# An If/Else on TensorE around the two matmul parts of each expert step: 192 or 128 token slots

## The chip, the cores and the metric

One core of one Trainium2 chip runs the kernel. The metric is the device time of one execution in microseconds; three timed runs of the kernel before are given, and one more execution was profiled. Engine names in the rows: PE is TensorE's matmuls, PEld its weight loads, DVE is VectorE, ACT ScalarE, POOL GpSimd, SP SyncE. A name with q (PEldq, ACTq) is what that engine's sequencer does by itself: waits, register loads, branches. L12 is line 12 of the kernel.

## What is computed

An attention stage (1152 rows of 512), a dense feed-forward layer, and then a mixture of eight experts, of which this change touches only the last:

```python
logits = x @ w_gate                          # 1152 tokens, 8 experts
expert_idx = np.argmax(logits, axis=1)
...                                          # disp[e, slot] = x[i]: the tokens of an expert in order
h = np.maximum(np.einsum('ecd,edf->ecf', disp, w1), 0.0)     # 512 -> 1024
y = np.einsum('ecf,efd->ecd', h, w2)                          # 1024 -> 512
out[i] = gate_w[i] * y[expert_idx[i], pos[i]]
```

An expert may hold up to 288 tokens. Working the reference's routing on its own inputs (seed 0) gives 138, 114, 113, 171, 190, 182, 128 and 116 tokens for experts 0 to 7.

## The kernel before, in words

All matrix products are in fp32 or in three products of split fp32 values (`mm3`: high by high, high by low, low by high). The experts run one after the other, each in eight steps; a step takes 128 of the 1024 hidden columns. Every expert is computed for 192 slots (`NW` = 128 + 64), whatever its number of tokens; slots above 192 have a block of their own at the end, under an If on all engines (L1132), which runs only if some expert has more than 192 tokens.

In a step TensorE does:

- `up(e, i)`: four fp32 matmuls of the step's slice of `w1b` with the gathered tokens `X`, 192 columns wide, into one of three PSUM banks `u`. In the trace each of them is two matmul records with two weight loads, so eight of each.
- `down(d, c)`, three steps behind (`LAG` = 3): the relu of an earlier step, `ht`, times the slice of the second weight. `mm3` into `y` for slots 0 to 127 is three matmuls of 512 columns; two more go into `z`, for the 64 slots above 127.
- at some steps `prep`: transposes of the next expert's gathered tokens (L930) that VectorE copies into `X`.

ScalarE and VectorE turn `u` into `ht` (`relu`, L1061 and L1063), split the second weights of the next expert into high and low parts (`split`, L235 and L236), and scale the finished `y` and `z` (`put_out`), which GpSimd scatters to the output. SyncE loads weights two to three experts ahead. The order on each engine is the order in which the main loop at the end of the kernel records the calls; `fills` is a table of extra calls after a step's matmuls. `r_final` (in expert 0) writes `flag_i`, and `get_flags` (expert 3) loads it into a register on every engine for the If at L1132.

The waits between engines are put in by the framework from the tiles that instructions read and write. An instruction with more than one wait gets wait instructions of its own ahead of it (EVENT_SEMAPHORE in the rows).

Of the kernel before, what the change touches and what calls it, by code (L numbers as in the profile page):

```python
# [1 line left out]

# [7 lines left out]
F32 = mybir.dt.float32  # L10
F32R = mybir.dt.float32r
I32 = mybir.dt.int32  # L12
# [3 lines left out]
ALU = mybir.AluOpType  # L16
AX = mybir.AxisListType

P = 128
# [5 lines left out]
PW = 384  # L25
N1 = 64
NW = P + N1
# [12 lines left out]
LAG = 3  # L40
# [2 lines left out]
_C = {}  # L43
_off = 0
for _name, _w in (("ident", 128), ("ml", KW), ("ml0", KW), ("ms", 54), ("tri", 128),
                  ("rev", 8), ("tok", 18), ("iota", PW)):
    _C[_name] = (_off, _w)
    _off += _w
CW = _off
# [3 lines left out]
def constants():  # L53
    c = np.zeros((P, CW), np.float32)

    def put(name, a):
        o, w = _C[name]
        c[: a.shape[0], o:o + w] = a

    i = np.arange(P)  # L60
    put("ident", np.eye(P))
    q = (i % QB)[:, None]
    col = np.arange(KW)[None, :]
    ok = (col > q) & (col <= q + STRIDE)
    put("ml", np.where(ok, 0.0, -8e9))
    put("ml0", np.where(ok & (col >= STRIDE), 0.0, -8e9))
    c54 = np.arange(54)[None, :]
    ok = (q // 18 == c54 // 18) & (c54 % 18 <= q % 18)
    put("ms", np.where(ok, 0.0, -8e9))
    put("tri", (i[:, None] < i[None, :]) * 1.0)  # L70
    put("rev", np.broadcast_to(8.0 - np.arange(8), (P, 8)))
    tok = np.empty((P, 9, 2))
    tok[:, :, 0] = i[:, None]
    tok[:, :, 1] = P * np.arange(9)[None, :]
    put("tok", tok.reshape(P, 18))
    slot = np.full(PW, -1.0)
    slot[0:NW] = np.arange(NW)
    slot[2 * P:PW - 32] = NW + np.arange(P - 32)
    put("iota", np.broadcast_to(slot, (P, PW)))
    return c  # L80
# [3 lines left out]
def tile_kernel(ctx, tc, cap, q, k, v, w_in, w_out, w_gate, w1, w2, consts, out):  # L84
    nc = tc.nc
# [3 lines left out]
    E, _, F = w1.shape  # L89
# [8 lines left out]
    cst = ctx.enter_context(tc.tile_pool(name="cst", bufs=1))  # L98
    dram = ctx.enter_context(tc.tile_pool(name="dram", bufs=1, space=bass.MemoryType.DRAM))
    rp = ctx.enter_context(tc.tile_pool(name="rp", bufs=3))  # L100
# [11 lines left out]
    def C(name):  # L112
        o, w = _C[name]
        return cs[:, o:o + w]
# [7 lines left out]
    idx_g = cst.tile([P, 3, E], I32, name="idx_g")  # L122
    idx_o = cst.tile([P, 3, E], I32, name="idx_o")
    gate = cst.tile([P, 3, E], F32, name="gate")
    flag_i = cst.tile([1, 1], I32, name="flag_i")
    x2d = dram.tile([NT, DM], F32, name="x2d")

    pp = ctx.enter_context(tc.tile_pool(name="ps", bufs=1, space=bass.MemoryType.PSUM))
# [5 lines left out]
    def psum(tag):  # L134
        name = rings[tag].pop(0)
        rings[tag].append(name)
        return pp.tile([P, 512], F32, tag=name, name=tag, bufs=1)
# [108 lines left out]
    def l1_mm(g, tb, c, tag):  # L246
        s, o = 2 * (g % 2), P * c
        hp = psum(tag)
        for kk in range(KC):
            mm3(hp[:, 0:TB], whi[s][:, kk, o:o + P], wlo[s][:, kk, o:o + P],  # L250
                xhi[:, kk, tb * TB:(tb + 1) * TB], xlo[:, kk, tb * TB:(tb + 1) * TB], kk == 0, kk == KC - 1)
            if kk < KC - 1:
                yield
        yield hp[:, 0:TB]
# [35 lines left out]
    def first_up():  # L290
        for c in range(2):
            for hp in l1_mm(0, 0, c, "f"):
                if hp is not None:
                    copies.append((nc.vector.tensor_copy if c else nc.scalar.copy, hb[c], hp))
                yield


    with ExitStack() as actx:
# [212 lines left out]
        up = first_up()  # L511
# [21 lines left out]
        for i in range(NGR):  # L533
# [6 lines left out]
            n, part = groups[i][:2]  # L540
# [21 lines left out]
        z = NGR - VL  # L562
        up = l1_mm(0, 0, 2, "f")
# [15 lines left out]
        hp = next(up)  # L579
# [7 lines left out]
        up = l1_mm(0, 0, 3, "acc")  # L587
# [212 lines left out]
    def r_final():  # L800
        extra = ohs
        cp = psum("m")
        for j, o in enumerate([cum] + extra):
            nc.tensor.matmul(cp[:, 0:E], lhsT=ones, rhs=o, start=j == 0, stop=j == len(extra))
        f = rp.tile([1, E], F32, name="flag", bufs=1)
        nc.vector.tensor_scalar(f, cp[0:1, 0:E], float(NW), None, op0=ALU.is_gt)
        fs = rp.tile([1, 1], F32, name="flags", bufs=1)
        nc.vector.tensor_reduce(out=fs, in_=f, axis=AX.X, op=ALU.add)
        nc.vector.tensor_copy(flag_i, fs)
        r_slot_ids(idx_o, idx)  # L810
# [69 lines left out]
    for n in range(4, nseq - 4):  # L880
        g, tb, c = seq[n]
# [167 lines left out]
            out=out, out_offset=bass.IndirectOffsetOnAxis(ap=idx_o[:n, ch, e:e + 1], axis=0), in_=y[:n], in_offset=None,  # L1049
            bounds_check=NT - 1, oob_is_err=False)  # L1050

    def up(e, i, n=NW):
        hp = psum("u")
        for kk in range(KC):
            nc.tensor.matmul(hp[:, 0:n], lhsT=w1b[e % 3][:, kk, P * i:P * i + P], rhs=X[e % 2][:, kk, 0:n],  # L1055
                             start=kk == 0, stop=kk == KC - 1)
        return hp
# [6 lines left out]
                                           op0=ALU.max, op1=ALU.subtract)  # L1064
        return t

    def down(e, i, t, y0, y1):
        j, c = 2 * (e % 2) + i // 4, i % 4
        for y in ((y1, y0) if i == 7 else (y0, y1)):
            if y is y0:  # L1070
                mm3(y0, t[:, 0:P], t[:, 2 * P:3 * P], whi[j][:, c], wlo[j][:, c], i == 0, i == 7)
            else:
                if i < 7:
                    nc.tensor.matmul(y1, lhsT=t[:, P:2 * P], rhs=whi[j][:, c], start=i == 0, stop=False)
                nc.tensor.matmul(y1[:N1], lhsT=t[:, P:NW], rhs=wlo[j][:, c], start=False, stop=False)
                if i == 7:
                    nc.tensor.matmul(y1, lhsT=t[:, P:2 * P], rhs=whi[j][:, c], start=False, stop=True)
# [6 lines left out]
    flags = []  # L1084

    def get_flags():
        flags.append(nc.values_load(flag_i[0:1, 0:1], min_val=0, max_val=E))

    fills = {}

    def fill(e, i, *fs):
        fills.setdefault((e, i), []).extend(fs)

    fill(0, 0, (r_match, BB))
    fill(0, 1, (r_index, BA))
    fill(0, 2, (r_index, BB), (gather, 1, 0), (gather, 1, 1), (r_final,))
    fill(0, 3, (r_weigh, BA))
    fill(0, 4, (r_weigh, BB))
    for e in range(E):
        fill(e, 3 if e == 0 else 0, (gather, e + 2, 0))  # L1100
        fill(e, 4 if e == 0 else 1, (gather, e + 2, 1))
        for h in range(4):
            fill(e, SPLIT_AT[h], (split, e + 1, h))
        fill(e, 5, (prep, e + 1, 0))
        fill(e, 6, (prep, e + 1, 1))
        for j in range(2):
            fill(e, 3 + 4 * j, (w1load, e + 3, j))
    fill(3, 0, (get_flags,))

    r_match(BA)  # L1110
    PARTS = ((NW, P, N1), (NW + N1, 0, P))
    ht, ys = {}, {}
    for s in range(8 * E + LAG):
        e, i = divmod(s, 8)
        if s < 8 * E:
            hp = up(e, i)
        d, c = divmod(s - LAG, 8)
        if s >= LAG:
            if c == 0:
                ys[d] = psum("y"), psum("z")  # L1120
            down(d, c, ht.pop((d, c)), *ys[d])
        for f, *args in fills.pop((e, i), []):
            f(*args)
        if s < 8 * E:
            ht[e, i] = relu(hp, PARTS)
        if s >= LAG and c == 7:
            y0, y1 = ys.pop(d)
            put_out(d, 1, y1)
            put_out(d, 0, y0)
    assert not fills, fills  # L1130

    with tc.If(flags[0] > 0):  # L1132
        n = ROWS[2]
        for e in range(E):
# [11 lines left out]
            for i in range(8):  # L1146
                t = relu(up(e, i, n), ((n, 0, n),), n)
                j, c = 2 * (e % 2) + i // 4, i % 4
# [32 lines left out]
```

## Time and profile before

| | |
|---|---|
| timed runs | 485.38, 487.12, 490.08 us (median 487.12) |
| the profiled execution | 483.33 us, of which the profile's span is 481.5 us |
| TensorE busy | 95% of the span, 3053 matmuls |
| VectorE, ScalarE, GpSimd busy | 59%, 42%, 25% |
| mean granted TensorE clock | 0.974 of full speed |
| expert steps in the trace | from 303.5 us (first `up`) to 470.3 us (last `down`) |

The span is told in us from its first instruction. A matmul's record is longer than the time after which the next one starts, since matmuls overlap; how long one takes up the engine is read from start to start.

### The profile page before, as it was taken

Reading aid. Unit: us, or ns where it says so; the run is one execution under the profiler, and the core shown is the slowest. Engines: PE = TensorE matmul, PEld = TensorE weight load, DVE = VectorE, ACT = ScalarE, POOL = GpSimd, SP = SyncE. Lnnn points to the kernel's source line nnn. Section 1 sums busy time; section 2 is a strip of 40 time slices with the busy share of each in tenths; the row PEclk is TensorE's granted clock in tenths of the full one; section 3 lists DMA queues with packets and bytes.
Section 4 is the critical chain, followed back from the end, with each engine's and each line's share of the span. In section 5 each row is a group of like instructions: output and inputs, shape, how many; then the busy total and the mean of one; then the engine's idle time right before and its main releaser. Section 6 shows DMA issues by size and latency. Waiting matters only on the chain. (4 is left out here: it accounts for less than half of the span.)

```text
span 481.5 us, 8430 instructions
## 1 busy us (share of the span) xinstructions
PE 455.1 (95%) x3053; PEld 390.3 (81%) x3055; DVE 285.5 (59%) x785; ACT 203.8 (42%) x521; POOL 120.5 (25%) x152
## 2 busy tenths in 40 slices
PE   8989898999998989999999999999999999999990
PEld 4667677898887879887998888988888888888880
DVE  3676999357878855787325686654454454455210
ACT  4576787245463432534244143323343342423211
POOL 1323553012332320323054215420220303101001
PEclk9987999999999999999999999799999999999996
DMA  7989747014243650446034013998767677200000
GB/s 158 217 211 231 179 144 241 29 44 132 87 132 96 211 176 0 138 169 219 0 88 152 3 67 114 372 305 286 244 200 225 232 247 232 76 1 31 1 23 24
DMA packets 52363, 69.04 MB, mean 143 GB/s; under 512 B 19800, under 2 KB 29272, under 8 KB 52316
## 3 DMA queue, kind: packets, MB, share of 16 engines
q1 hardware_dynamic: 50268, 63.18, 42.8%
q0 software_dynamic: 2048, 5.26, 3.6%
q8 instruction: 26, 0.43, 0.4%
q14 instruction: 21, 0.17, 0.1%
HBM read 61.60 MB, written 7.86 MB: 144 GB/s over the span
## 5 line engine op out<-in xcount | busy, mean ns | idle before, releaser
L1055 PE MATMUL u<-X,w1b 128*128 128x192 f32 x512 | 95.7, 331 | 0.0
L1055 PEld LDWEIGHTS u<-X,w1b 128*128 128x128 f32 x512 | 86.1, 192 | 6.3
L198 POOL TENSOR_TENSOR wlo<-w,whi 128x512 fp32r<-128x512 f32 x32 | 44.2, 1383 | 117.4 <-DVE gl L267 79.5
L1061 ACT ACTIVATE ht<-u 128x192 fp32r<-128x192 f32 x64 | 21.2, 331 | 105.0 <-PE u L1055 65.2
L161 PE MATMUL acc<-whi,gh 128*128 128x512 f32 x144 | 58.2, 404 | 4.7 <-DVE x L288 4.6
L161 PE MATMUL h<-xhi,whi 128*128 128x384 f32 x176 | 59.8, 340 | 0.0
L163 PE MATMUL h<-xhi,wlo 128*128 128x384 f32 x176 | 59.4, 338 | 0.0
L162 PE MATMUL h<-xlo,whi 128*128 128x384 f32 x176 | 59.4, 338 | 0.0
L163 PE MATMUL acc<-whi,gl 128*128 128x512 f32 x144 | 56.9, 395 | 0.0
L162 PE MATMUL acc<-wlo,gh 128*128 128x512 f32 x144 | 56.7, 394 | 0.0
L1063 DVE SCALAR_TENSOR_TENSOR ht<-u,ht 128x64 fp32r<-128x64 f32 (+1 forms) x128 | 26.9, 252 | 46.7 <-ACT ht L1061 46.7
L266 ACT CAST gh<-g 128x384 fp32r<-128x384 f32 x48 | 24.6, 513 | 63.0 <-DVE g L259 63.0
L1048 POOL DMA_INDIRECT out_dram<-y,idx_o x16 | 15.5, 966 | 124.1 <-DVE y L1045 81.7
L259 DVE TENSOR_TENSOR g<-h,g 128x384 f32<-128x384 f32 x44 | 24.4, 554 | 35.5 <-ACT g L258 35.5
L267 DVE TENSOR_TENSOR gl<-g,gh 128x384 fp32r<-128x384 f32 x48 | 26.7, 557 | 25.7 <-ACT gh L266 25.5
L258 ACT ACTIVATE g<-h 128x384 f32<-128x384 f32 x44 | 21.5, 488 | 48.4 <-PE h L163 48.2
L189 DVE SCALAR_TENSOR_TENSOR wsb<-raw,wsb 128x512 uint32<-128x512 uint32 x32 | 39.3, 1228 | 1.0
L236 DVE TENSOR_TENSOR wlo<-raw,whi 128x1024 fp32r<-128x1024 f32 x28 | 34.2, 1222 | 9.2 <-ACT whi L235 9.2
L419 ACT ACTIVATE pr<-sc,st 128x54 f32<-128x54 f32 (+1 forms) x84 | 28.8, 344 | 17.6 <-DVE st L416 17.6
L161 PEld LDWEIGHTS acc<-whi,gh 128*128 128x128 f32 x144 | 27.0, 188 | 10.0 <-ACT w L186 5.5
L161 PEld LDWEIGHTS h<-xhi,whi 128*128 128x128 f32 x176 | 33.1, 188 | 1.9
L162 PEld LDWEIGHTS h<-xlo,whi 128*128 128x128 f32 x176 | 33.1, 188 | 1.8
(198 smaller groups left out, 854.7 us busy)
## 6 DMA issues: line engine op xcount, KB each, us to landing
w1b<-in_moe_w_dram SPq DMA_DIRECT2D x32, 512.0 KB
raw<-in_moe_w_dram SPq DMA_DIRECT2D x32, 512.0 KB
raw<-in_moe_w_in_dram SPq DMA_DIRECT2D x16, 512.0 KB
raw<-in_moe_w_out_dram SPq DMA_DIRECT2D x16, 512.0 KB
out_dram<-zw SPq DMA_DIRECT2D x1, 2304.0 KB
x2d<-x SPq DMA_DIRECT2D x2, 768.0 KB
vl<-in_v_dram SPq DMA_DIRECT2D x4, 288.0 KB
kr<-in_k_dram SPq DMA_DIRECT2D x4, 288.0 KB
```

The costliest lines, as they stand in the source:

```text
L161: nc.tensor.matmul(o, lhsT=ah, rhs=bh, start=first, stop=False)
L162: nc.tensor.matmul(o, lhsT=ah, rhs=bl, start=False, stop=False)
L163: nc.tensor.matmul(o, lhsT=al, rhs=bh, start=False, stop=last)
L189: nc.vector.scalar_tensor_tensor(out=u, in0=top, scalar=0x80000000, in1=u, op0=ALU.bitwise_and, op1=ALU.bitwise_or)
L198: nc.gpsimd.tensor_sub(wlo[slot][:, k], t, whi[slot][:, k])
L236: (nc.vector if e else nc.gpsimd).tensor_sub(wlo[slot][:, k], raw, whi[slot][:, k])
L259: nc.vector.tensor_mul(a, h, a)
L266: nc.scalar.copy(gh, a)
L267: nc.vector.tensor_sub(gl, a, gh)
L419: nc.scalar.activation(out=pr[:, a], in_=sc[:, a], func=AF.Exp, scale=-1.0, bias=st[:, 0, a:a + 1], accum_out=st[:, 1, a:a + 1])
L1055: nc.tensor.matmul(hp[:, 0:n], lhsT=w1b[e % 3][:, kk, P * i:P * i + P], rhs=X[e % 2][:, kk, 0:n], start=kk == 0, stop=kk == KC - 1)
L1063: nc.vector.scalar_tensor_tensor(out=t[:, o:o + m], in0=hp[:, c:c + m], scalar=0.0, in1=t[:, c:c + m], op0=ALU.max, op1=ALU.subtract)
```

## The change

`flag_i` gets two words. Each is a sum of powers of two, one bit for each expert: the first has the bit of an expert with more than 128 tokens, the second that of one with more than 192. TensorE alone loads the first word (`get_wides`, after step 5 of expert 0). From expert 1 on, the up part and the down part of each step stand in an If on that expert's bit, with an Else: the If part is the old one, the Else part has `up` at 128 columns and `down` without the two matmuls into `z`. Expert 0 stays as it was. The three `u` banks and `z` are now allocated once instead of at each step. ScalarE, VectorE and GpSimd still do 192 slots; what they compute from the unfilled ones is not written to the output.

```diff
-        f = rp.tile([1, E], F32, name="flag", bufs=1)
-        nc.vector.tensor_scalar(f, cp[0:1, 0:E], float(NW), None, op0=ALU.is_gt)
-        fs = rp.tile([1, 1], F32, name="flags", bufs=1)
+        f = rp.tile([1, 2, E], F32, name="flag", bufs=1)
+        for j in range(2):
+            nc.vector.scalar_tensor_tensor(out=f[:, j], in0=cp[0:1, 0:E], scalar=float((P, NW)[j]), in1=C("bit")[0:1],
+                                           op0=ALU.is_gt, op1=ALU.mult)
+        fs = rp.tile([1, 2], F32, name="flags", bufs=1)
...
-    def up(e, i, n=NW):
-        hp = psum("u")
+    def up(e, i, n=NW, hp=None):
+        hp = next(us) if hp is None else hp
...
-    def down(e, i, t, y0, y1):
+    def down(e, i, t, y0, y1, more=True):
...
-            else:
+            elif more:
...
+    def get_wides():
+        wides.append(nc.tensor.value_load(flag_i[0:1, 0:1], min_val=0, max_val=2 ** E - 1))
+
+    def either(e):
+        if e == 0:
+            yield 1
+        else:
+            with tc.If((wides[0] & (1 << e)) > 0) as cmp:
+                yield 1
+            with cmp.Else():
+                yield 0
...
+    fill(0, 5, (get_wides,))
...
-    ht, ys = {}, {}
+    ht, ys, y1 = {}, {}, psum("z")
+    us = itertools.cycle([psum("u") for _ in range(3)])
     for s in range(8 * E + LAG):
         e, i = divmod(s, 8)
+        d, c = divmod(s - LAG, 8)
         if s < 8 * E:
-            hp = up(e, i)
-        d, c = divmod(s - LAG, 8)
+            hp = next(us)
+            for case in either(e):
+                up(e, i, NW if case else P, hp)
         if s >= LAG:
             if c == 0:
-                ys[d] = psum("y"), psum("z")
-            down(d, c, ht.pop((d, c)), *ys[d])
+                ys[d] = psum("y"), y1
+            t = ht.pop((d, c))
+            for case in either(d):
+                down(d, c, t, *ys[d], more=case)
```

How this moves instructions is shown at three places of the built programs. The first is TensorE in step 3 of expert 1, in the kernel before: the up part, and then the down part of step 0 of the same expert (`u`, `y` and `z` are PSUM tiles, `whi` and `wlo` the split second weights).

```order
L1055 MATMUL u<-X_3335,w1b_1520 128x192 [waits DVE_49,Activation_49]
L1055 MATMUL u<-X_3335,w1b_1520 128x192 x3
L161 MATMUL y<-whi_1515,ht 128x512
L162 MATMUL y<-wlo_1516,ht 128x512
L163 MATMUL y<-whi_1515,ht 128x512
L1074 MATMUL z<-whi_1515,ht 128x512 [waits DVE_49]
L1075 MATMUL z<-wlo_1516,ht 64x512
```

The same up part on TensorE in the changed kernel: a register operation and a compare-and-branch ahead, both forms of the part, each closed by a branch.

```order
L1102 REGISTER_ALU
L1102 COMPARE_AND_BRANCH
L1059 MATMUL u<-X_3335,w1b_1520 128x192 [waits DVE_49,Activation_49]
L1059 MATMUL u<-X_3335,w1b_1520 128x192 x3
L1102 UNCONDITIONAL_BRANCH
L1059 MATMUL u<-X_3335,w1b_1520 128x128 [waits DVE_49,Activation_49]
L1059 MATMUL u<-X_3335,w1b_1520 128x128 x3
L1102 UNCONDITIONAL_BRANCH
```

The waits are the same in both forms; one of the two groups of four matmuls runs. The down part that follows it on TensorE in the changed kernel:

```order
L1102 REGISTER_ALU
L1102 COMPARE_AND_BRANCH
L163 MATMUL y<-whi_1515,ht 128x512
L164 MATMUL y<-wlo_1516,ht 128x512
L165 MATMUL y<-whi_1515,ht 128x512
L1078 MATMUL z<-whi_1515,ht 128x512 [waits DVE_49,Activation_49]
L1079 MATMUL z<-wlo_1516,ht 64x512
L1102 UNCONDITIONAL_BRANCH
L163 MATMUL y<-whi_1515,ht 128x512
L164 MATMUL y<-wlo_1516,ht 128x512
L165 MATMUL y<-whi_1515,ht 128x512
L1102 UNCONDITIONAL_BRANCH
```

There are 112 such pairs, 56 around up parts and 56 around down parts. The second place is VectorE in the steps of expert 1 in the kernel before (relu pairs, one split, the copy into `X`):

```order
L1063 SCALAR_TENSOR_TENSOR ht<-u,ht 128x64 [waits Activation_49]
L1063 SCALAR_TENSOR_TENSOR ht<-u,ht 128x128
L236 TENSOR_TENSOR wlo_1518<-raw,whi_1517 128x1024 [waits DMAHW6_49,Activation_49]
L1063 SCALAR_TENSOR_TENSOR ht<-u,ht 128x64 [waits Activation_49]
L1063 SCALAR_TENSOR_TENSOR ht<-u,ht 128x128
L932 COPY X_3335<-m 128x4x128 [waits PE_49]
```

and in the changed kernel, where VectorE's own work stands in the same order with a branch to the next piece of the program at each of TensorE's pairs:

```order
L238 TENSOR_TENSOR wlo_1518<-raw,whi_1517 128x1024 [waits DMAHW6_49,Activation_49]
L1102 UNCONDITIONAL_BRANCH x2
L1067 SCALAR_TENSOR_TENSOR ht<-u,ht 128x64 [waits Activation_49]
L1102 UNCONDITIONAL_BRANCH
L1067 SCALAR_TENSOR_TENSOR ht<-u,ht 128x128
L1102 UNCONDITIONAL_BRANCH
L936 COPY X_3335<-m 128x4x128 [waits PE_49]
```

ScalarE, GpSimd and SyncE have the same 112 branches. Each goes to the instruction that stands next on that engine.

## Rows read from the trace of the kernel before

**Rows 1.** Busy us by engine in windows of 20 us, then granted clock, DMA share, GB/s

```profile
360.00:380.00 20.00, 20.00 (x110) 17.52 (x109) 9.24 (x22) 7.76 (x14) 3.29 (x4) 1.00 0.75 241
440.00:460.00 20.00, 20.00 (x110) 17.51 (x109) 6.18 (x20) 4.96 (x11) 1.90 (x2) 1.00 0.03 13
```

**Rows 2.** Timeline of PE, one step: start us, length us, line, operation

```profile
332.88 1.46 PE L1055 MATMUL u<-X,w1b 128*128 128x192 f32 x8
334.05 0.53 PE L161 MATMUL y<-whi,ht 128*128 128x512 f32 x1
334.41 0.39 PE L162 MATMUL y<-wlo,ht 128*128 128x512 f32 x1
...
335.11 0.39 PE L1075 MATMUL z<-wlo,ht 128*64 128x512 f32 x1
335.34 1.46 PE L1055 MATMUL u<-X,w1b 128*128 128x192 f32 x8
```

**Rows 3.** Timeline of PE, the transposes of `prep` and what follows

```profile
337.79 0.60 PE L930 MATMUL m<-cs,xg 128*128 128x128 f32 x4
338.22 1.47 PE L1055 MATMUL u<-X,w1b 128*128 128x192 f32 x8
```

**Rows 4.** Records of tile z: duration min/median/max ns, first and last start us

```profile
L1075 PEld LDWEIGHTS z<-wlo,ht x64: 133/135/137, 311.4 to 468.7; 128*64 128x64 f32 x64
L1074 PEld LDWEIGHTS z<-whi,ht x56: 187/187/188, 311.1 to 468.3; 128*128 128x128 f32 x56
```

**Rows 5.** Records of lines 1055 and 1087 near 361 to 368 us, as rows 4

```profile
L1055 PEldq EVENT_SEMAPHORE  x1: 946/946/946, 361.5 to 361.5; - x1
...
L1055 PEldq EVENT_SEMAPHORE  x2: 51/51/51, 365.8 to 368.2; - x2
...
L1087 PEldq TENSOR_LOAD <-flag_i x1: 482/482/482, 363.3 to 363.3; - x1
...
L1087 SPq FUSED_REGOPS  x1: 197/197/197, 367.1 to 367.1; - x1
```

**Rows 6.** Timeline of PE around that load

```profile
363.15 0.52 PE L161 MATMUL y<-whi,ht 128*128 128x512 f32 x1
...
364.44 1.46 PE L1055 MATMUL u<-X,w1b 128*128 128x192 f32 x8
...
366.88 1.46 PE L1055 MATMUL u<-X,w1b 128*128 128x192 f32 x8
```

**Rows 7.** Records of line 1132, the If at the end, as rows 4

```profile
L1132 POOLq EVENT_SEMAPHORE  x5: 17/43/43, 474.5 to 477.0; - x5
...
L1132 PEldq COMPARE_BRANCH  x1: 3771/3771/3771, 466.6 to 466.6; - x1
L1132 ACTq COMPARE_BRANCH  x1: 50/50/50, 470.3 to 470.3; - x1
L1132 DVEq COMPARE_BRANCH  x1: 72/72/72, 470.3 to 470.3; - x1
L1132 PEldq EVENT_SEMAPHORE  x1: 51/51/51, 470.4 to 470.4; - x1
...
L1132 ACTq EVENT_SEMAPHORE  x1: 17/17/17, 473.6 to 473.6; - x1
L1132 POOLq COMPARE_BRANCH  x1: 45/45/45, 474.0 to 474.0; - x1
```

**Rows 8.** Timeline of the last matmul and the last ScalarE instruction

```profile
469.86 0.39 PE L163 MATMUL y<-whi,ht 128*128 128x512 f32 x1
470.31 0.69 ACT L1047 ACTIVATE y<-y,gate 128x512 f32<-128x512 f32 x1
```

**Rows 9.** The page: TensorE's busy time and instructions; the queue that brings instructions

```profile
PE 455.1 (95%) x3053; PEld 390.3 (81%) x3055; DVE 285.5 (59%) x785; ACT 203.8 (42%) x521; POOL 120.5 (25%) x152
...
q8 instruction: 26, 0.43, 0.4%
```

**Rows 10.** ScalarE's waits ahead of relu, 320 to 465 us, as rows 4

```profile
L1061 ACTq EVENT_SEMAPHORE  x57: 1297/2377/2982, 319.2 to 463.3; - x57
```

More of the change, by code (lines that the diff above doesn't have):

```diff
@@ L1 @@
+import itertools
 from contextlib import ExitStack
@@ L45 @@
 for _name, _w in (("ident", 128), ("ml", KW), ("ml0", KW), ("ms", 54), ("tri", 128),
-                  ("rev", 8), ("tok", 18), ("iota", PW)):
+                  ("rev", 8), ("bit", 8), ("tok", 18), ("iota", PW)):
     _C[_name] = (_off, _w)
@@ L70, in constants @@
     put("tri", (i[:, None] < i[None, :]) * 1.0)
+    put("bit", np.broadcast_to(2.0 ** np.arange(8), (P, 8)))
     put("rev", np.broadcast_to(8.0 - np.arange(8), (P, 8)))
@@ L124, in tile_kernel @@
     gate = cst.tile([P, 3, E], F32, name="gate")
-    flag_i = cst.tile([1, 1], I32, name="flag_i")
+    flag_i = cst.tile([1, 2], I32, name="flag_i")
     x2d = dram.tile([NT, DM], F32, name="x2d")
@@ L1086, in get_flags @@
     def get_flags():
-        flags.append(nc.values_load(flag_i[0:1, 0:1], min_val=0, max_val=E))
+        flags.append(nc.values_load(flag_i[0:1, 1:2], min_val=0, max_val=2 ** E - 1))
+    wides = []
+    def get_wides():
[8 more added lines that the diff above has]
+                yield 0
     fills = {}
```

## The prediction, made before the changed kernel ran

> **What bounds the kernel now.** I read the page first, then the busy time by windows, then TensorE's timeline of one step, and last the records of what sequencers do by themselves. The windows over the experts show TensorE busy for 20.00 of 20 us at a granted clock of 1.00, beside 9.2 us of VectorE and 7.8 us of ScalarE while weights still load, and less afterwards [rows 1]. ScalarE stands 1.3 to 3.0 us ahead of each relu waiting for `up` [rows 10]. So from 303.5 to 470.3 us the time is what TensorE needs, and work taken from it shortens the span one for one, as long as nothing starves it.
>
> A step starts `up` at 332.88 us and the next at 335.34, so it takes 2.46 us. Its five down matmuls follow each other at 0.93 / 4 = 0.232 us (334.41 to 335.34, four slots) [rows 2]. That leaves 2.46 - 5 x 0.232 = 1.30 us for the eight `up` records, 0.163 us each at 192 columns.
>
> **What is removed.** The reference's routing gives 128 tokens or fewer to experts 1, 2, 6 and 7; the test is "more than 128", so expert 6 with exactly 128 takes the short form too. That is 4 x 8 = 32 steps.
>
> - Down: two matmuls of 0.232 us less, 0.46 us a step.
> - Up: no record of this form with 128 columns is in the trace. By the columns it would take 0.163 x 128 / 192 = 0.109 us. Near it are the 128-column transposes, 0.43 / 4 = 0.108 us each [rows 3]. The weight loads do not get shorter. A load of 64 weight columns is recorded with 135 ns, one of 128 with 187 [rows 4], so 64 columns take about 52 ns and 128 about 105, which just fits beneath 0.109; the rest of the record overlaps its neighbours. The bounds are 0.163 (loads are already the limit, no gain) and 0.109. I take 0.109: 8 x 0.054 = 0.43 us a step.
>
> Together 0.89 us a step, 32 x 0.89 = 28.5 us (14.8 at the worse bound of `up`). A short step takes 1.56 us.
>
> **What is added, and what hides it.** Everything new runs in TensorE's sequencer, which feeds the engine. How far it runs ahead is in the rows. At 361.5 us it stood for 946 ns in a wait for the `up` that the engine began at 364.44. Released at 362.45, it passed that `up` and one down part, 16 + 10 matmuls and loads, and began the register load at 363.3 [rows 5]. That is 0.85 us / 26 = 33 ns an instruction. The engine was then only in the previous down part, which began at 363.15 [rows 6], so the sequencer was over 30 records or some 3 us ahead. The next waits are 2.4 us apart, one step [rows 5]: it is held at the engine's pace by how much it may queue. The load of 482 ns in its path cost nothing, since `up` starts lie 2.44 us apart across it [rows 6]. The new load in expert 0 (482 ns, and a register operation like SyncE's of 197 ns [rows 5]) is hidden by the same lead; its flag is older than a VectorE result that TensorE waits for just before.
>
> Per If there is a register operation, a compare-and-branch, and in the long form a jump over the Else. Their prices on TensorE are not in the trace. The register operation lies between 51 ns (a wait record) and 197 ns [rows 5]. A branch lies between the 45 to 72 ns of its own record on three engines and the 0.5 us from GpSimd's branch at 474.0 to its next record at 474.5 [rows 7]. So a short step's If costs 0.1 to 0.7 us. The sequencer then needs 22 x 0.033 + 0.05 for a wait + 2 x (0.1 to 0.7) = 1.0 to 2.2 us against 1.56 us of matmuls. A long step needs 26 x 0.033 + 0.05 + 2 x (0.15 to 1.0, with the jump too) = 1.2 to 2.9 us against 2.46. I take the middle for the short step, about 1.5, and the lower half for the long one: both just hidden. At the upper bounds the loss would be 32 x 0.64 = 20 us in short steps and 24 x 0.44 = 11 us in long ones (experts 3 to 5), together a net loss of about 2 us.
>
> [...]
>
> The code grows. 6108 matmuls and loads came in 26 transfers on the instruction queue [rows 9], 235 a transfer. A step of both forms is about 58 instructions, so 56 steps take some 14 transfers. About 40% of that code is jumped over (26 of 58 in a short step, 22 in a long one), so 5 or 6 of the 14 borders are crossed by a jump. If such a jump found its code missing it would wait: ScalarE's branch at 470.3 has its next record at 473.6, 3.3 us later, though its last instruction ended at 471.0 [rows 7, 8]. With 2 to 3 us queued, each would expose about 1 us. The bounds are 0 and 6 x 3.8 = 23 us; I take 2 us.
>
> The branches on the other engines go to their next instruction and run while these engines wait [rows 10]. VectorE has 9.2 us of work in 20 us [rows 1], about 9.5 us an expert, and a short expert lasts 8 x 1.56 + 0.8 for `prep` = 13.3 us, so VectorE does not become the bound; uncovered, its excess would be seen as waits of `down` on `ht`. Weights: the DMA share is 0.75 at 20 us an expert [rows 1], so 13.3 us would ask for more than all of it. Experts 1 and 2 draw on loads issued two experts ahead, and long experts follow, so nothing is late; the cover gone, it would cost up to 2 us an expert. The second flag adds one tiny VectorE operation.
>
> **Sum.** 483.3 - 28.5 + 2 = 456.8 us for an execution like the profiled one. The median shown, 487.1, is 3.8 us above the profiled one; I carry that over: 460.6, say 461 us.
>
> **The rivals.**
>
> *TensorE's branch waits until its queue has run empty (slower).* For it: the compare-and-branch on TensorE is recorded with 3771 ns, from 466.6 to 470.35, and the last matmul began at 469.86 with a record of 0.39 us, so it ended at 470.25 [rows 7, 8]. On ScalarE, VectorE and GpSimd the record is 45 to 72 ns, and ScalarE's branch at 470.3 was over while its instruction ran to 471.0. Against it: this branch jumps over the whole block for slots above 192, and 3.77 us is also about the hole that ScalarE's jump left (3.3 us), so it can be a wait for code; and the register load did not empty the queue. Price: at each If the tail of a matmul (0.39 - 0.23 = 0.16), the step from branch to next record (0.06) and a weight load that nothing covers (0.19) stand open, 0.41 us. 112 x 0.41 = 46 us, so 483.3 - 28.5 + 46 = 501, or 505 us against the median. If the 48 jumps of the long forms drain as well, another 20 us: 525. It decides from 28.5 / 112 = 0.25 us an If on.
>
> *Branches or code transfers cost near their upper bounds.* For it: the 0.5 us on GpSimd and the 3.3 us hole. Against it: GpSimd had a scatter on its hands, and jumps here skip 6 to 16 instructions. Net gain of 5 to 17 us: 470 to 482 us, and up to 490 with all of them at their bounds.
>
> [...]
>
> *It saves less than it says.* If `up` is bound by its loads the gain is 14.8 - 2 = 13 us, 474; if expert 6 counts one token more, 7 us are lost, 468.
>
> **How the numbers follow.** Forecast, 455 to 469 us: 0.55. High branch or code costs, 470 to 482: 0.12; the same down to no gain, within 1%: 0.05. Smaller saving, 468 to 475: 0.06. Draining, 495 us and above: 0.22, of which about half above 510. One per cent, 4.9 us, is about what a measurement of this kernel can tell from no change. So faster 0.73, same 0.05, slower 0.22. The range goes from 455 to 510 and leaves out some 0.05 below and 0.11 above; both signs lie in it, and the forecast's own range is 455 to 470.
>
> **What would show it.** Right: `up` of experts 1, 2, 6 and 7 as eight 128-column records 0.11 us apart, three down matmuls 0.23 apart, steps of about 1.6 us there and 2.46 in experts 3 to 5, TensorE still busy throughout, branch records near 0.1 us. Draining would show as branch records of microseconds that end with the matmul before them and a gap of some 0.4 us at every If, in experts 3 to 5 too. Missing code would show as few gaps of 1 to 4 us, each beside a transfer on the instruction queue. A bound by loads would show as 128-column `up` records 0.16 apart.

## The result, and the profile after

Four runs of the changed kernel gave 459.01 us (455.65 to 459.69) beside 486.25 us before on the same chip: ratio 0.950, 95% interval 0.940 to 0.960. The profiled execution took 455.65 us, its span 453.6 us, 27.9 us less than before. The forecast was 461, with 455 to 470 as its own range. Where the runs of a kernel lie further apart (481.93 to 495.57 us with far jumps), its ratio leaves out those that took longer at a lower granted clock (there the two of 495.5 and 495.57 us, at 0.93 and 0.94 against 0.97 and 0.96).

First the page of after, the rows that answer to [rows 9], and one window by engine (columns as in [rows 1]):

```profile
PE 428.3 (94%) x2991; PEld 369.0 (81%) x2991; DVE 284.9 (63%) x786; ACT 203.2 (45%) x521; POOL 122.1 (27%) x152
...
q8 instruction: 33, 0.54, 0.5%
```

```profile
340.00:360.00 20.00, 20.00 (x129) 18.18 (x128) 13.05 (x31) 11.28 (x20) 4.81 (x5) 1.00 1.01 354
```

TensorE lost 27 us of work and is still busy for 20.00 of 20 us at a granted clock of 1.00. VectorE rose from 9.2 to 13 us a window and the DMA share from 0.75 to 1.01, and TensorE waits for neither. Next, TensorE's timeline of expert 1 (start, length, line, operation): its first `up`, and then its first step with both parts short (in the three steps between, the down part is still that of expert 0, and long).

```profile
321.56 1.06 PE L1059 MATMUL u<-X,w1b 128*128 128x128 f32 x8
...
327.69 1.05 PE L1059 MATMUL u<-X,w1b 128*128 128x128 f32 x8
328.50 0.48 PE L163 MATMUL y<-whi,ht 128*128 128x512 f32 x1
328.81 0.40 PE L164 MATMUL y<-wlo,ht 128*128 128x512 f32 x1
329.05 0.39 PE L165 MATMUL y<-whi,ht 128*128 128x512 f32 x1
329.28 1.05 PE L1059 MATMUL u<-X,w1b 128*128 128x128 f32 x8
```

A short step takes 329.28 - 327.69 = 1.59 us against 2.46 [rows 2]: three down matmuls of 0.23 us, and 0.89 us for the rest, 0.111 us an `up` record. The branches stand in the records of the If's line 1102 and of the last If, now line 1156 (minimum, median and maximum ns, first and last start):

```profile
L1102 PEldq COMPARE_BRANCH  x160: 67/179/339, 318.8 to 437.6; - x160
...
L1156 PEldq COMPARE_BRANCH  x1: 3477/3477/3477, 439.1 to 439.1; - x1
```

The 160 are 112 comparisons and the 48 jumps at the end of long arms. A comparison that falls through into the long arm takes 67 to 77 ns, a taken one mostly 210 to 220, a jump mostly 169 to 180. The last If is the row that spoke for the worst rival. It now runs from 439.1 to 442.6 us, but the last matmul is long over:

```profile
440.56 0.39 PE L165 MATMUL y<-whi,ht 128*128 128x512 f32 x1
```

It ended at 440.95, 1.6 us before the branch did. With both arms long (the first experiment below) the order is the other way round: the branch ends at 472.2, and the last matmul at 472.51.

```profile
L1156 PEldq COMPARE_BRANCH  x1: 3399/3399/3399, 468.8 to 468.8; - x1
...
472.12 0.39 PE L165 MATMUL y<-whi,ht 128*128 128x512 f32 x1
```

So this branch does not wait for the last matmul, and that both ended together before [rows 7, 8] was chance.

For all kernels below I compare one stretch of the trace, from the first `up` of expert 1 to the start of the last matmul; expert 0, whose first step varies by up to 1.3 us from one execution to the next, is left out.

| kernel | stretch, us | against after | ratio to before (95%) |
|---|---|---|---|
| before | 146.77 | +27.77 | 1 |
| after | 119.00 | 0 | 0.950 (0.940 to 0.960) |
| both arms long | 146.74 | +27.74 | 1.005 (0.999 to 1.010) |
| no If, forms fixed | 119.00 | 0.00 | 0.937 (0.929 to 0.945) |
| up alone | 133.71 | +14.71 | 0.974 (0.966 to 0.981) |
| down alone | 131.99 | +12.99 | 0.975 (0.966 to 0.983) |
| four Ifs a step | 119.34 | +0.34 | 0.955 (0.951 to 0.959) |
| eight Ifs a step | 216.89 | +97.89 | 1.153 (1.147 to 1.158) |
| up at 96 columns | 118.95 | -0.05 | 0.953 (0.948 to 0.958) |
| all experts short | 98.23 | -20.77 | 0.912 (0.908 to 0.915) |
| an If with an empty arm, six times | 124.15 | +5.15 | 0.956 (0.950 to 0.963) |
| second transposition in an If | 120.15 | +1.15 | 0.950 (0.946 to 0.955) |
| the same, one record kept | 118.43 | -0.57 | 0.940 (0.935 to 0.945) |
| far jumps, eight times | 147.61 | +28.61 | 1.001 (0.993 to 1.008) |

### The profile page after: what moved, and what is told of

Its sections match the earlier page's. It is cut to its first block, busy times and chain, and to the rows that moved or that the text cites. A ratio compares the mean times of both kernels' runs of the same rounds, so it can differ in the third digit from the quotient of the medians.

```text
span 453.6 us, 8618 instructions
## 1 busy us (share of the span) xinstructions
PE 428.3 (94%) x2991; PEld 369.0 (81%) x2991; DVE 284.9 (63%) x786; ACT 203.2 (45%) x521; POOL 122.1 (27%) x152
## 5 line engine op out<-in xcount | busy, mean ns | idle before, releaser
L1059 PE MATMUL u<-X,w1b 128*128 128x192 f32 (+1 forms) x512 | 82.4, 305 | 0.0
L1059 PEld LDWEIGHTS u<-X,w1b 128*128 128x128 f32 x512 | 76.1, 192 | 5.2
L1052 POOL DMA_INDIRECT out_dram<-y,idx_o x16 | 16.5, 1032 | 98.0 <-DVE y L1049 61.4
```

## The experiments

### What the Ifs cost by themselves

Both arms made long, so that every branch is there and nothing is saved:

```diff
-                up(e, i, NW if case else P, hp)
+                up(e, i, NW, hp)
-                down(d, c, t, *ys[d], more=case)
+                down(d, c, t, *ys[d])
```

> Both arms of every If hold the long form (192 columns, five down matmuls), so the 112 Ifs and the jumps stay and no matmul is saved. Theory (branches run in TensorE's sequencer ahead of the engine): no change against before, within 1%, with long steps of 2.45 us in all experts and no gap on TensorE. Rival (each If costs the engine something that the saved matmuls paid for): slower by what the Ifs cost, 112 x 0.1 to 0.4 us = 11 to 45 us.

The forms fixed when the kernel is built, with no branch at all (this only fits these inputs):

```diff
-            with tc.If((wides[0] & (1 << e)) > 0) as cmp:
-                yield 1
-            with cmp.Else():
-                yield 0
+            yield 0 if e in (1, 2, 6, 7) else 1
```

> The form of each expert is written down when the program is made (experts 1, 2, 6 and 7 short), with no If around the step parts: the changed kernel without its control flow. Theory: the same as the changed kernel within 1%, about 0.945 to 0.955 of before, short steps of 1.58 us. Rival (branches or jumped code borders still cost): faster than the changed kernel by 3 to 10 us, 0.93 to 0.94 of before, short steps below 1.58 us or fewer gaps.

Measured: 485.16 us, ratio 1.005, the stretch 0.03 us from that of before; and 453.03 us, ratio 0.937, the stretch equal to that of after to 0.01 us. Timelines of both, an `up` and the next, the first pair with both arms long:

```profile
330.29 1.47 PE L1059 MATMUL u<-X,w1b 128*128 128x192 f32 x8
...
332.74 1.46 PE L1059 MATMUL u<-X,w1b 128*128 128x192 f32 x8
```

```profile
327.30 1.05 PE L1059 MATMUL u<-X,w1b 128*128 128x128 f32 x8
...
328.89 1.05 PE L1059 MATMUL u<-X,w1b 128*128 128x128 f32 x8
```

2.45 us and 1.59 us: the steps of before and of after. So two Ifs a step cost TensorE nothing, with and without a jump. The ratio of 0.937 lies where I had put the rival, though its interval overlaps that of after, and the profiled span without Ifs is 2.8 us shorter than that of after. None of it lies in the stretch: the kernel reached expert 1 0.4 us earlier, and its tail, from the start of the last matmul to the end of the span, was 2.4 us shorter. Most of it is one row, ScalarE's scaling of the last `z`, in after and then without Ifs:

```profile
440.54 0.69 ACT L1048 ACTIVATE y<-z,gate 64x512 f32<-64x512 f32 x1 [1.93 <-PE y L163]
```

```profile
438.19 0.69 ACT L1048 ACTIVATE y<-z,gate 64x512 f32<-64x512 f32 x1
```

Without Ifs `z` is scaled 2.0 us before the last matmul starts (440.18). With them the scaling starts only as the last matmul does, released by a matmul of the last down part, although a short one writes nothing into `z`. So the Ifs do cost the profiled execution some 2 us, once, at its end and off TensorE. The tail has a second cost, told at the end of the account below.

### The two savings apart

```diff
-                down(d, c, t, *ys[d], more=case)
+                down(d, c, t, *ys[d])
```

> Only the up part has a short form; both arms of the down part are the long one. Theory: short steps of 2.05 us, a gain of 32 x 0.41 = 13 us, about 0.973 of before. Rival (the weight loads limit up, so most of the gain is from down): a gain under 5 us.

```diff
-                up(e, i, NW if case else P, hp)
+                up(e, i, NW, hp)
```

> Only the down part has a short form; both arms of the up part are 192 columns wide. Theory: short steps of 1.99 us, a gain of 32 x 0.46 = 15 us, about 0.970 of before. With the run of up alone the two gains should add up to the 28 us of the changed kernel; a rival in which one part hides behind the other would show a sum that differs by more than 3 us.

Measured: 470.72 and 471.92 us, ratios 0.974 and 0.975. `up` alone takes 13.06 us from the stretch of before, 0.408 us a step; down alone 14.78, 0.462 us a step; together 27.84, and the change took 27.77. They add up. In the timelines a step with `up` alone short (first pair) takes 2.05 us, one with down alone short 1.99:

```profile
331.43 1.06 PE L1059 MATMUL u<-X,w1b 128*128 128x128 f32 x8
...
333.48 1.06 PE L1059 MATMUL u<-X,w1b 128*128 128x128 f32 x8
```

```profile
331.89 1.46 PE L1059 MATMUL u<-X,w1b 128*128 128x192 f32 x8
...
333.88 1.46 PE L1059 MATMUL u<-X,w1b 128*128 128x192 f32 x8
```

### How many Ifs a step can bear

Four pairs of arms a step: `up` cut behind its second chunk, and in the same way down behind its second record.

```diff
...
-            for case in either(e):
-                up(e, i, NW if case else P, hp)
+            for kks in ((0, 1), (2, 3)):
+                for case in either(e):
+                    up(e, i, NW if case else P, hp, kks)
...
```

> Four pairs of arms in a step where the change has two: the up record list is cut after chunk 1 and the down list after the second record, so the same matmuls run in the same order, with twice the branches. If an If were free wherever it stands, short steps stay at 1.585 us and the kernel at 459 us. If TensorE's step is the longer of what its engine works and what its sequencer needs, the price per If shows once the sequencer is the longer one: after shows a comparison not taken at about 0.07 us, a taken one or a jump at 0.17 to 0.22 us, an arithmetic instruction at 0.036 us ahead of some, so about 0.33 us for each If of a short step with what lies around it and about 0.46 us for each of a long one; with 22 other instructions at the 33 ns of the prediction a short step would need 0.73 + 4 x 0.33 = 2.05 us against 1.585 (32 steps: 15 us), a long one 0.9 + 4 x 0.46 = 2.7 us against 2.45 (24 steps: 6 us), about 480 us. In both cases no wait for TensorE's own queue to empty: gaps stay below 0.5 us each.

Measured: 460.37 us, ratio 0.955; the stretch is 0.34 us longer. My sum said 2.05 us a short step, and it stayed at 1.58 to 1.59, as the timeline shows:

```profile
341.83 1.05 PE L1059 MATMUL u<-X,w1b 128*128 128x128 f32 x8
...
343.41 1.05 PE L1059 MATMUL u<-X,w1b 128*128 128x128 f32 x8
```

Eight pairs: each chunk, each record into `y` and the records into `z` in an If of their own.

```diff
...
-            for case in either(e):
-                up(e, i, NW if case else P, hp)
+            for kk in range(KC):
+                for case in either(e):
+                    up(e, i, NW if case else P, hp, (kk,))
...
-            for case in either(d):
-                down(d, c, t, *ys[d], more=case)
+            for part in range(4):
+                for case in either(d):
+                    down(d, c, t, *ys[d], more=case, part=part)
```

> Eight pairs of arms in a step: each of the four up chunks, each of the three records into y and the records into z stand in an If of their own. With four pairs a step the matmuls were still unmoved, and the branch rows stood 0.39 us apart, four of them just inside a step of 1.585 us. If an If costs TensorE's sequencer about 0.33 us with the arithmetic ahead of it and only becomes visible when the sequencer's sum is the longer one, eight of them need 2.6 to 3.1 us: short steps go from 1.585 to 2.6 to 3.1 us (32 steps: 32 to 48 us) and long steps, whose arms also end in a jump (0.17 us more), from 2.45 to 3.5 to 4.3 us (24 steps: 25 to 44 us): 515 to 550 us. If branches are free at any number: 459 us.

Measured: 558.36 us, ratio 1.153, past even the dearer case. TensorE now waits for its own sequencer (PEq as releaser). First the records of the If's line, with four Ifs and with eight, each within a short step, then TensorE's timeline of a long one with eight:

```profile
L1106 PEldq ALU_OP  x4: 36/36/36, 340.7 to 341.8; - x4
```

```profile
L1104 PEldq ALU_OP  x7: 36/36/36, 338.9 to 341.2; - x7
L1104 PEldq COMPARE_BRANCH  x6: 208/208/208, 339.0 to 340.9; - x6
```

```profile
385.12 2.08 PE L1059 MATMUL u<-X,w1b 128*128 128x192 f32 x8 [0.95 <-PEq L1104]
...
389.05 2.01 PE L1059 MATMUL u<-X,w1b 128*128 128x192 f32 x8 [0.53 <-PEq L1104]
```

The first and the seventh of seven Ifs in a row lie 2.3 us apart, 0.38 us an If, of which the two records fill 0.25. With four Ifs a step, whose `up` arms hold two matmuls instead of one, they stand as close (340.7 to 341.8 for four of them). A step also has a wait ahead of its `up`, some 0.1 us, so that four Ifs need at least 1.64 us, more than a short step of 1.59, and eight need 3.2. That four a step cost next to nothing is owed to the lead: in expert 7 the sequencer took 12.3 us for seven steps (28 Ifs, from the first to the last start of 29), the engine 11.1, and the sequencer's lead on the engine's `up` fell from 2.0 to 0.9 us.

```profile
L1106 PEldq ALU_OP  x29: 36/36/36, 429.2 to 441.5; - x29
...
431.24 1.05 PE L1059 MATMUL u<-X,w1b 128*128 128x128 f32 x8
...
442.35 1.05 PE L1059 MATMUL u<-X,w1b 128*128 128x128 f32 x8
```

More short steps in a row would, by this, use the lead up; no run here has them. With eight Ifs a step, part of the 3.5 to 3.9 us that most short steps took is a cost that I had not reckoned with: the fourth down arm is empty in the short form, and the trace has 32 semaphore instructions on that line, one a short step. From that If to the next it mostly takes 0.65 to 0.7 us instead of 0.38. The next experiment has it alone.

### An empty arm

This was meant as a test of far jumps: an If that is never entered, over 300 matmuls.

```diff
+            if 1 <= e <= 6 and i == 2:
+                with tc.If(wides[0] > 255):
+                    for _ in range(75):
+                        up(e, i, P, hp)
```

> The change as it is, and ahead of the up records of step 2 of experts 1 to 6 one more If that is never entered, whose body holds 300 matmul instructions, so that the jump passes over code that has not been loaded. The Ifs of the change jump over at most a dozen instructions, and the last If of the kernel, which jumps far, showed 3.5 us. If it is the distance (code that must come by DMA), each of the six jumps holds TensorE's sequencer 3 to 4 us, beside a transfer on the instruction queue; the records that it had queued ahead (about 3 us) cover most of it, and a gap of 0.3 to 1.5 us in TensorE is left at each: 2 to 9 us in all, 461 to 468 us. If an If costs the same however far it goes, no gap: 459 us. If the sequencer doesn't run ahead at all across a branch, 3.5 us at each: 480 us.

The register is declared as at most 255, so the comparison could be decided when the program was built; neither it nor the matmuls are in the program. What was left at each place is a branch to the next instruction and a semaphore instruction that waits until TensorE has given all its signals (in the trace it starts 0.04 us after TensorE's last matmul has ended) and then raises the same count for the body that was skipped. So it says nothing on far jumps, but it prices that instruction. Measured: 461.30 us, ratio 0.956, the stretch 5.15 us longer, 0.86 us each. Records of the If's line, and the timeline around the first one:

```profile
L1139 PEldq EVENT_SEMAPHORE  x6: 51/51/51, 325.7 to 419.3; - x6
```

```profile
325.22 0.40 PE L1079 MATMUL z<-wlo,ht 128*64 128x512 f32 x1
326.39 1.13 PE L1059 MATMUL u<-X,w1b 128*128 128x128 f32 x8 [0.77 <-ACT whi L237]
```

The last matmul ends at 325.62, the semaphore instruction follows at 325.7, and the next matmul starts 1.17 us after the last instead of 0.23. The releaser named there (ScalarE) is inferred; I do not take it for the cause, since six such gaps stand at the six places of this instruction. At each of them, and at all 35 others in the two kernels with eight Ifs and with the empty arm below, the semaphore instruction starts 0.04 us after the end of TensorE's last matmul. This is the drain that I had feared of the branch; in these runs it stands only at arms without a signal, and the If's line of after has no semaphore instruction.

The same appears where one would like to use an If: around the second transposition of `prep`, which a short expert doesn't need (its tile now stays the same from expert to expert).

```diff
...
-            nc.tensor.transpose(tp[:, kk * n:(kk + 1) * n], xg[:n, kk * P:(kk + 1) * P], ident[:n, :n])
+        for case in either(e) if ch == 1 and e > 1 else (1,):
+            for kk in range(KC if case else 0):
+                nc.tensor.transpose(tp[:, kk * n:(kk + 1) * n], xg[:n, kk * P:(kk + 1) * P], ident[:n, :n])
```

> The change, and the transposition of the second token chunk (four records, 64 tokens) of experts 2 to 7 put in an If of the same kind; a short expert then leaves it out, and the tile keeps what the last long expert left. In after this transposition takes 0.43 us of TensorE where it stands (the step with it is 2.02 to 2.08 us against 1.59). Experts 2, 6 and 7 are short: three times 0.4 to 0.5 us less, 1.2 to 1.5 us, about 457.6 us, a ratio 0.997 to after and about 0.947 to before. If the If there makes TensorE wait for its own queue instead, as a jump whose other side signals differently would, three to six gaps of about 0.9 us take the gain back: 459 to 463 us.

And as before, but with the last of the four records kept in the short arm:

```diff
-            for kk in range(KC if case else 0):
+            for kk in range(0 if case else KC - 1, KC):
```

> As the kernel that puts the second transposition in an If, but the arm of a short expert keeps the last of the four records, so that both arms end with a record that signals. With the empty arm the trace shows, at each of the three short experts, a semaphore instruction of the If that waits for TensorE's own count 0.1 us after its last matmul ended, and the steps with it took 2.43, 3.15 and 2.75 us against 2.07, 2.94 and 2.07 in after. If the empty arm is the cause (its signal has to be given by an instruction that first waits for TensorE to finish), there is no such instruction here and no gap: these three steps take 0.3 to 0.35 us less than in after, 1.7 to 1.8, 2.6 and 1.7 to 1.8 us, and the kernel about 1 us less than after, ratio to before about 0.945 to 0.95. If any If at this place makes TensorE wait, the steps stay above those of after and the kernel at 460 us.

Measured: 460.25 us with the empty arm, ratio 0.950, the stretch 1.15 us longer than in after; 456.90 us with one record kept, ratio 0.940 (0.935 to 0.945), the stretch 0.57 us shorter. The records of the If's line with the empty arm, then the timelines around the transposition, the empty arm first:

```profile
L1108 PEldq EVENT_SEMAPHORE  x3: 51/51/51, 339.5 to 429.3; - x3
```

```profile
339.05 0.40 PE L165 MATMUL y<-whi,ht 128*128 128x512 f32 x1
340.12 1.13 PE L1065 MATMUL u<-X,w1b 128*128 128x128 f32 x8 [0.67 <-DVE wlo L238]
```

```profile
336.19 0.40 PE L165 MATMUL y<-whi,ht 128*128 128x512 f32 x1
336.52 0.27 PE L940 MATMUL p<-cs,xg 64*128 64x64 f32 x1
336.72 1.16 PE L1065 MATMUL u<-X,w1b 128*128 128x128 f32 x8
```

With nothing in the arm 1.07, 0.90 and 1.40 us pass between the two matmuls at the three places, and the saving turns into a loss. With one record there the line has no semaphore instruction, and the step with it takes 1.89 us against 2.07 in after, three times 0.19 us less: the mechanism as expected, the gain smaller than the 0.3 to 0.35 that I gave it, since the first record of such a group costs more than each that follows (the step is 0.30 us longer with one record than with none, and 0.06 us longer with each further one). This version is ahead of after in its trace by these 0.57 us; the times' intervals overlap, and by them alone it could be level.

### Far jumps

The long arm of `up` repeated 75 times in two steps of each short expert, so that eight taken branches go over 300 matmuls, with the same signals on both sides.

```diff
-                up(e, i, NW if case else P, hp)
+                for _ in range(75 if case and e in (1, 2, 6, 7) and i in (2, 7) else 1):
+                    up(e, i, NW if case else P, hp)
```

> In steps 2 and 7 of experts 1, 2, 6 and 7 the long arm of the up part holds its records 75 times over (300 matmuls); these experts are short, so that the long arm is jumped over and never entered: eight jumps over code that has not been loaded, with the same signals on both sides. If it is the distance that costs (code that must come by DMA), each such jump shows as a branch row of 3 to 4 us beside a transfer on the instruction queue, as the last If of the kernel does, and with about 1 to 3 us of records queued ahead a gap of 0.5 to 2.5 us in TensorE is left at each: 4 to 20 us in all, 463 to 479 us. If the next code is fetched ahead whatever the branch does, or an If costs the same however far it goes, no gap: 459 us.

Measured: ratio 1.001 (0.993 to 1.008), 481.93 us for the profiled execution. The whole gain is gone: the stretch is 28.61 us longer, 3.6 us a jump on average, above the 0.5 to 2.5 us that I gave. The page's instruction queue, the branch record of the first jump, and TensorE around it:

```profile
q8 instruction: 49, 0.80, 0.7%
```

```profile
L1102 PEldq COMPARE_BRANCH  x1: 6567/6567/6567, 321.4 to 321.4; - x1
```

```profile
324.23 0.40 PE L1079 MATMUL z<-wlo,ht 128*64 128x512 f32 x1
328.12 1.52 PE L1059 MATMUL u<-X,w1b 128*128 128x128 f32 x8 [3.49 <-issue]
...
329.87 0.63 PE L1081 MATMUL z<-whi,ht 128*128 128x512 f32 x1
330.30 0.63 PE L163 MATMUL y<-whi,ht 128*128 128x512 f32 x1
```

Sixteen transfers more than the 33 of after, two a jump; the eight long branch records take 3.8 to 6.6 us. TensorE went on for 3.2 us (321.4 to 324.6) on what was queued, then stood for 3.5. What I had missed comes behind that: the down matmuls after the gap start 0.43 us apart instead of 0.23, and the window by engine shows a lower granted clock there.

```profile
324.00:328.00 4.00, 0.63 (x3) 0.13 (x1) 1.57 (x3) 0.83 (x1) 0.00 (x0) 1.00 0.92 326
328.00:332.00 4.00, 3.88 (x16) 3.43 (x16) 1.17 (x3) 1.20 (x3) 0.00 (x0) 0.59 0.34 126
```

After a window with 0.63 us of matmuls the granted clock is 0.59 instead of 1.00. The gaps behind the eight long branch records are 1.4 to 3.9 us from start to start. Two more belong to the jumps: 2.8 us at 428.74, in the middle of the `up` that the fifth jump led to, with a transfer on the instruction queue at 429.2, and 1.3 us at 465.45, behind a branch record of 2.4 us. The ten make 21.3 us beyond the usual 0.23 each. The other 7.3 us lie nearly all in the steps behind four of them, where the granted clock was lower (the 4 us from 328, from 342, from 431 and from 444 us show 0.57 to 0.59); behind the other gaps it stayed at 1.00. How long the gap was does not tell which: one of 2.2 us was followed by such a stretch, one of 2.7 us was not.

### What would bind next

The short arm of `up` with fewer columns (it leaves out the slots from 96 on of the short experts, where stale values go on):

```diff
-                up(e, i, NW if case else P, hp)
+                up(e, i, NW if case else 96, hp)
```

> The short arm of the up part at 96 columns instead of 128; columns 96 to 127 of the short experts are left out of the up part, and stale values go on from there. The prediction took the up record by its columns, 0.109 us at 128. If columns set it, 96 of them cost 0.082 us, the short step falls from 1.585 us by 0.43 to 1.36 to 1.38 us and the kernel by up to 13 us to 446 us, unless the two Ifs' own price in the sequencer (about 1.4 us a step by the estimate from the branch records of after) ends it there. If the load of the weights (128x128, 4 bytes) sets it, the record stays at 0.109 us and the step at 1.58 us: 459 us.

A threshold that makes every expert from 1 to 7 short (it leaves out the tokens above 128 of experts 3, 4 and 5):

```diff
-scalar=float((P, NW)[j])
+scalar=float((9 * P, NW)[j])
```

> The threshold of the first flag is raised to 1152 tokens, so that all experts 1 to 7 take the short arms; the second chunks of experts 3, 4 and 5 (tokens above 128) are left out. If TensorE alone sets the time, the 24 long steps fall from 2.45 to 1.585 us: 20 us less, about 438 us. If the weights' transfers and VectorE's splitting of them, which the prediction named as hidden at a price of up to 2 us an expert, become the bound once seven short experts stand one behind the other, expert 3 and those behind it take more than 14.7 us each: up to 2 us x 5 more, 440 to 448 us, with TensorE waiting for a DMA or VectorE.

Measured: 459.45 us, ratio 0.953, the stretch 0.05 us from that of after; and 439.19 us, ratio 0.912. With 96 columns, the timeline of one step:

```profile
331.95 1.02 PE L1059 MATMUL u<-X,w1b 128*128 128x96 f32 x8
332.76 0.48 PE L163 MATMUL y<-whi,ht 128*128 128x512 f32 x1
...
333.54 1.03 PE L1059 MATMUL u<-X,w1b 128*128 128x96 f32 x8
```

`up` takes 0.81 us to the first down matmul and the step 1.59 us, as with 128 columns. It isn't the sequencer, which in after passed a whole short step in 1.0 us (424.0 to 425.0). What is left is the load of the 128 x 128 weights at 0.111 us, and another part of the trace of after agrees: the router's matmuls of only 24 columns, with weights of that size, start 0.11 us apart too (line 654, seven of them from 292.85 to 293.51). With all of experts 1 to 7 short, a window by engine (columns as above):

```profile
340.00:360.00 20.00, 20.00 (x142) 18.07 (x141) 13.89 (x35) 12.09 (x22) 5.75 (x6) 1.00 1.01 359
```

The 24 steps of experts 3 to 5 lose 20.77 us, 0.865 us each, every expert in the middle takes 13.7 us, and TensorE does not wait, with the DMA share at 1.01 and VectorE at 14 of 20 us. So the cover that I had named, long experts behind the short ones, was not needed for the seven experts here.

## Why the prediction was right, step by step

- **The bound.** Right: time taken from TensorE's records shortened the stretch one for one, in every kernel here that took some (27.77 us for the change, 13.06 and 14.78 for its two parts).
- **Down, 0.46 us a step.** Measured 0.462.
- **Up, 0.43 us a step.** Measured 0.408: a record of 0.111 us, not 0.109. The estimate of about 105 ns for the load, which "just fits beneath 0.109", was the right rival at a slightly low price; by all that is left the load sets the record, and 96 columns gain nothing. Both savings together: 28.5 us foretold, 27.8 measured.
- **What the sequencer costs.** Its result, just hidden, held with more room than I thought. "33 ns an instruction" is the term that failed: an If costs 0.38 us (0.47 in a long arm) whether one matmul lies in its arm or two, so the matmul and load instructions added next to nothing here. The 0.85 us for 26 of them in [rows 5] was an upper bound that I took for a price. A short step needs at most 1.0 us of the sequencer and not 1.5. The branch's range of 0.1 to 0.7 us held its 0.38. The lead of some 3 us is borne out: 3.2 us of work were left when the sequencer stood in the first far jump. It is not a constant, though: in after the first If of a step ran 0.6 to 3.4 us ahead of the engine's `up`.
- **Branch records near 0.1 us.** Half right. The trace of after has 67 to 77 ns for a comparison that falls through and mostly 210 to 220 for one that is taken, and an If with what surrounds it, at 0.38 us, costs more than either.
- **New code, 2 us.** Not there in the stretch: 33 transfers instead of 26, and the stretch is that of the kernel without Ifs. The jumps of the change skip 6 to 16 instructions, and no border among them showed. The wait for code itself is real and dearer than its price: eight jumps over 300 matmuls cost 28.6 us, with 16 more transfers on the instruction queue and branch records of 3.8 to 6.6 us.
- **VectorE and the weights.** Right that both are hidden; the price of up to 2 us an expert did not come up, even with seven short experts in a row.
- **The sum.** 456.8 us foretold for a profiled execution, 455.65 measured: 0.7 us too much saving and 2 us too much for code. What lies outside the stretch had no term. Expert 1 was reached 1.5 us earlier than before, with a granted clock of 0.98 instead of 0.95 in the first 100 us, and the tail took 1.5 us more; that these two cancelled was luck. The 3.8 us carried over to the median made 461 against 459.01, within what executions differ by.
- **The rival with 0.22, a branch that drains.** It fell: no gap of 0.4 us at any If, equal stretches with and without branches, and a last If that outlasted the last matmul by 1.6 us. What does drain is the semaphore instruction that the program gets where one arm has no signal to give, at 0.86 us in place of the rival's 0.41. The change's arms both end in a record that signals.
- **The tail.** From the start of the last matmul to the end of the span 13.1 us pass in after and 11.6 before. The kernels here with a short down arm in branches show 12.0 to 13.4, those with a long one 11.5 and 11.6, that with fixed forms 10.7. Against before, 1.3 us of it is GpSimd's wait ahead of its last scatter, 3651 ns against 2317. In after three of the 48 packets of the scatter before it moved only at 444.8 us, as an instruction transfer begun at 443.3 ended; the other 45 had moved by 444.0. The first row is that wait in after and the second the one of before; then come the instruction queue (q8) and the scatter's (q0, packets first) from 443.0 to 444.7 us, and the scatter's from 444.7 to 444.9:

```profile
L1052 POOLq EVENT_SEMAPHORE  x1: 3651/3651/3651, 442.1 to 442.1; - x1
L1048 POOLq EVENT_SEMAPHORE  x1: 2317/2317/2317, 471.2 to 471.2; - x1
...
q8 instruction: 1, 0.02, 5.4%
q0 software_dynamic: 45, 0.00, 1.3%
...
q0 software_dynamic: 3, 0.00, 1.7%
```

Before, all 48 moved within 0.2 us, with no such transfer under way. Five other kernels with a short down arm in branches show the same three late packets at the end of a transfer. That the transfer held them up fits all six; no run moved it away, so this stays open, as does what puts the transfer there.

## What to carry to other kernels

Here TensorE's sequencer ran 0.6 to 3.4 us ahead of its engine and paid for the Ifs, at 0.38 us each, 0.47 in a long arm. With two a step it needed at most 1.0 us against the 1.59 of a short step, and the stretch stayed as it was to 0.01 us; with four, 1.64 us by the estimate above, it grew by 0.34 us while the lead fell from 2.0 to 0.9 us in expert 7; with eight it grew by 97.89. So count the Ifs of a step against its work. Keep both arms short and let both end in an instruction that signals; an empty arm made TensorE wait for its own queue, at 0.86 us each, and a jump over 300 matmuls took 3.6 us on average. Look at the end of the kernel too: there a result that the short form doesn't touch was released only by the last down part, some 2 us later than without Ifs. Before cutting columns further, see what the weight load takes: here an `up` record took 0.111 us at 128 columns, and 96 took 0.05 us from the stretch.

## What the runs showed of the hardware that was not expected

- Issuing matmuls cost TensorE's sequencer almost nothing beside branches: 0.38 us an If, with one matmul in the arm or with two.
- After a gap of 3.5 us TensorE ran at a granted clock of 0.59 over the next 4 us. Of the 28.6 us that eight far jumps cost, a quarter came behind the gaps, four of which were followed by such a stretch.
- With four Ifs a step the sequencer was the slower of the two for seven steps and no step showed it: its lead paid, 2.0 us at first and 0.9 at the end.
- One If had a branch record of 3.5 us though its engine was idle for the last 1.6 of them: the length of that record said nothing on a drain until it was set beside the end of the matmul ahead of it.
